# Attention to the first 512 tokens: value products split between the windows and the sums of v; third chunk reads keys that are already on chip

## The chip, the cores and the metric

The kernel runs on one core of a Trainium2 chip. The metric is the device time of one execution in microseconds (us). The engines are TensorE (PE, its weight loads shown apart as PEld), VectorE (DVE), ScalarE (ACT), GpSimd (POOL) and SyncE (SP). Here SP issues all the DMAs. Each engine works through its own list of instructions in order; semaphores make one wait for another.

## The reference

Attention over a local window and over block summaries, then a softplus feed-forward. Everything is float32.

```python
# q, k, v: (4, 8, 768, 64); w_in: (512, 2048); w_out: (2048, 512)
block, window = (32, 16)
nb = S // block                                                   # 24 blocks
k_sum = k.reshape(B, H, nb, block, D).max(axis=3)
v_sum = v.reshape(B, H, nb, block, D).mean(axis=3)
scores_l = scale * np.matmul(q, k.transpose(0, 1, 3, 2))          # masked to |i - j| < 16
scores_s = scale * np.einsum('bhsd,bhnd->bhsn', q, k_sum) + np.log(block)
...
a = softmax(np.concatenate([scores_l_m, scores_s], axis=-1))
x = np.matmul(a, np.concatenate([v, v_sum], axis=2))              # to (3072, 512)
h = x @ w_in
out = (np.maximum(h, 0.0) + np.log1p(np.exp(-np.abs(h)))) @ w_out
```

## The kernel before

**Tiling.** The 3072 tokens (4 batches of 768) are 12 chunks of 256. Heads go in pairs (`hp`, four of them), two heads on the 128 partitions; a unit of attention is one chunk and two head pairs (`NG = 2`), so there are two units a chunk. Within a unit there are 4 windows of 64 queries; each sees 96 keys around it (`KW`) and the 24 summaries (`NB`) of its batch, 120 in all (`KS`).

**A unit of attention** (`attention`): PE makes scores (`sc`, L582), DVE adds the mask and finds maxima (L595), ACT takes exponentials (L603), DVE inverts the sums (L610, L611), DVE or POOL normalizes (L616), the probabilities are transposed into `pT`, and PE multiplies them with v into `xo` (L673). ACT and DVE then write `xo` as a high and a low part, `xh` and `xl` (L689, L693).

**The first two chunks** (512 tokens of batch 0) are done before all else, by `FirstPlaces`, with `by_pe` true: their transposes are made on PE (`pt`, L629) and copied by ACT into `pT` (L633). Their keys lie on chip whole (`kf`, `Sums.declare_first`), so scores are made in two pieces, 96 columns from the keys and 24 from the block maxima `ks`. The sums of v are made on PE (`vt`, L403) and scaled by ACT into 24 rows at partitions 96 to 119 of `vn` (L416). The tile of v for these units, `first`, holds for each window the 96 rows of v at partitions 0 to 95; a DMA for each head pair (`load_sums`, L536) spreads the 24 rows of sums, once for each of the 8 windows, to partitions 96 to 119 of `first`. A value product then takes all 120 rows at once. `vs` is a second copy of the sums, by four small DMAs (`keep_first`, L422), for the third chunk.

**All later chunks** use `Places`: windows of k and v are loaded by DMA for each unit (L474, L483), the maxima are copied behind the keys of each window by DVE or ACT (L490), the sums of v are loaded by DMA (L500), and the transpose goes through DVE and a DRAM buffer `squares` (L642, L650, L654). The third chunk, the last of batch 0, is among these.

**The feed-forward** takes groups of two chunks (the third and the last chunk alone). For each of 16 slices `f` of the hidden width PE makes `ph` (L804), ACT the softplus (L824, L828), DVE the low part `gl` (L832), PE the product with w_out into `po` (L841). The weights are split into a high and a low part on chip, by some eight steps on DVE, ACT and POOL for each slice (L735 to L775). The buffers of the 16 slices serve as scratch first: 6 and 7 hold `vn`, 8 to 11 `first`, 14 and 15 the resident keys `kf`. At the start PE also runs 40 products without use (`warm`, L915).

**The order.** Every step is a task with an index. `SEQUENCE` lists the tasks in the order of their issue; this order is each engine's list, SP's DMAs included. A letter behind an index names another way of doing it (another engine). The numbers in `order.add` (an engine and a time) served to make the sequence; at run time only the sequence counts.

Of the kernel before, what the change touches and what calls it, by code (L numbers as in the profile page):

```python
# [10 lines left out]
F32 = mybir.dt.float32  # L11
# [136 lines left out]
2 160 43 45 68 64 51 133 0 53 161a 3 151 4 44 5 6 162 46 47 7 165a 100 163 72 164 49 166 55 8 73 1 9 167 96 10  # L148
11 138 142 134a 168 74 84 135 57 136 137 52 59 85 139 12 54 101 152a 132 61 75 13 86 140a 14 66 76a 50 141a 70
56 48 77 156 65 15 153 16 69 154 143a 104 189 87 147 144 145 78 79 146 190 17 80 58 155 105 148 60 62 149 88a 63  # L150
116 106 67 150a 18 117 71 19 157 20 21 169 22 23 170 24 158a 25 98 118 26 159 102 27 28 107 29 108a 30 97 31 103
32 33 191 99 81 195 192 179 89 180 193 91 90 34 194 92 35 199 82 119 93 171a 83 196 388 94 109 36 128 95 110 111
37 120a 112 129 38 197 390 172 113 391 175 198 131 121 130 123 122 173 39 124 40 389 174 41 114 200 42 125 181a
387 115 176 309 126 185 127 182 396a 310 219 177 183 220 184 239 318 311 240 178 319 312 186 313 399 320 321 314
414 201a 209 315 187a 415 325 188 210 413 205 202 229 269 203 221a 204 316 225 317 249 222 326 322 206 400 331
417 289 245 223 207 416 224 323 230 332 333 208 327 290 324 226 328 241a 334 337 279 227 242 259 243 401 329 244
228 343 422a 402 211a 403a 338 330 212 213 425 214 344 335 345 246 404 339 215 336 340 405 602 235 426 341 216
247 346 427 342 248 347 217a 584 604 218 348 392 393 395 349 394 428 588 429 406 585 397 231a 408 355 407 398
350 232 409 233 603 234 250 351 353 356 589 236 357 352 586 610a 605 358 410 601 430 237 354 418 419 411 238 359
424 431 412 251a 270 587a 361 423 255 252 590 253 613 362 254 432 367 420 614 434 256 363 421 435 433 364 615  # L160
628 360 257a 365 258 591a 594 366 373 368 598 616 260 369 371 374 370 375 595a 436 376 599 592 372 437 280 275
438 378 377 439 617 381a 382 593 383 379 440 627 441 445 265 630 442 606 271 631 380 446 295 272 451 273 447 596
274 443 452 299 453 444 629 448 276 449 454 457 597 277 463 458 278 450 459 464 455 465 460 636a 456 384 261 461
385 262 469 386 608 466 263 639 470 618 285 475 654 471 264 655 619 462 476 653 472 467 266 477 640 291a 468 473
478 474 641 481 292 658 267a 487 293 294 479 482 600 661 296 483 480 675 488 485 484 676 489 300 490 493 297 268
620 677 623 499 642 494 622 643a 680a 495 281a 486 298a 496 491 644 508 662 645 500 282 305 492 283 683 509 284
501 497 804 510 502 607 286 301a 498 511 805 516 609 621 612 663 302 806 287a 504 288 512 503 303 812a 522 304
517 505a 306 506a 518 513 523 507 519 807 514 524 611 307 528 525 803 664 308 665a 515 666 534 542 529 530 667
531 684 624 520 685 632 635 646 637 815 633 634 521 649 648 526 647 625 638 535 626 830 527 686 832 687a 546 532
536 831 833 537 688 650 550 651 668 656 652 657 533 551 816 671 838a 660 552 556 669 553 670 541 557 659 558 539  # L170
817 559 689 538 548 829 562 543 544 540 545 672 554 818 678 673 819a 690 555 563 679 841 691 547 681 564 560 565
692 674 693 561 682 566 820 549 568 857 574 569 570 571 567 575 694 576 577 572 695 808 814 696 573 578 873 842
811 697 809 810 858a 580 821 705 698 855 699 843 700 581 701 702 822 579 874 711 582 825 823 706 844 583 845a
872 876 856 875 703 712 813 704 713 707 709 708 859 714 717 846 847 867 824 723 718 860 861 710 724 719 715 725
720 868 716 881 865 862a 721 726 729 884 730 731 826 732 866a 722 827 834 848 735 869 835 828 849 885 863 837
851 727 736 899 836 737 840 886 738 728 839 870a 741 901 850 902 864 900 898 907 733 742 887 888a 747 743 744
889 753 748 749 734 910 750 852 911 739 877 740 754 853 745 755 912 756 871 746 854 882 759 890 879 913 765 760
914a 891 915 880 761 893 762 892 751 883 894 878 771 766 916 767 752 757 768 895 772 773 758 903 896 904 897 763
906 774 917 918 919 764 920 905 769 908 909 770 1031 1035 1032 775 1030 776 921 777 1033 922 1034 923 1036 1037
783 778 779 780 789 784 785 786 924 790 791 792 1038 932 1039 1053 1054 1052 1057 1040 781 782 787 925 1041 1042  # L180
788 926 793 933 927 794 934 797a 795 798 1043 796 799 928 800a 801 1044 929 935 802 938 930 939 931 940 1045
1060 941 1046 1047 1048 936 1061 937 1062 942 943 1049 1063 944 1055 1050 1064a 1074 1075 1083a 1051 1077 1065
1076 1078 950 945 1056 1066 1058 946 1059 947 948 951 952 953 1086 956 1067 1087 1068 1069 1070 1088 962 949 957
954 1089 1090a 1091 958 955 963 960 959 1092 964 1100 965 1101 1109a 961 1071 968 1072 1079 1081 1073 1093 1094
1095 1096 974 969 1080 1082 970 1084 971 1085 980 975 1103 1102 976 1104 977 1097 966 1105 1098 1107 1099 1106
1108 1112 981 1110 982 1111 967 1113 1232 972 1236 983 1114 973 978 979 984 1115 1116a 1117 985 986 1233 1118
1237 1234 1238 992 987 1119 1120 988 1121 989 1122 990 993 994 995 998 1235a 1239a 1242 1004 999 1000 1246 1001
1249 1250 1258 1251 1010 1005 1253 1006 1252 1243 991 996 1247 1007 1240 1016 1011 1012 1244 1248 1241 1261 997
1262 1002 1013 1263 1245 1003 1008 1009 1017 1014 1264 1265a 1266 1018 1015 1123 1019 1267 1275 1276 1284 1020
1124 1277 1021 1024 1125 1279 1278 1022 1025 1254 1023 1027 1026 1126 1268 1028a 1269 1270 1271 1029 1255 1134  # L190
1127 1257 1256 1128 1259 1129 1260 1287 1135 1136 1130 1288 1131 1132 1137 1289 1133 1138 1272 1139 1280 1281
1273 1290 1140 1283 1291a 1282 1285 1274 1286 1292 1146 1141 1293 1302 1306 1303 1142 1301 1143 1144 1147 1148
1149 1294 1152 1295 1296 1297 1158 1153 1154 1155 1298 1159 1160 1309 1304 1299 1305 1300 1307 1145 1310 1308
1150 1161 1311 1151 1156 1157 1162 1312 1313a 1163 1314 1164 1315 1324 1328 1325 1323 1170 1165 1316 1166 1317
1318 1167 1168 1171 1319 1172 1173 1176 1320 1177 1178 1331 1326 1321 1179 1327 1322 1329 1169 1332 1330 1174
1333 1175 1180 1181 1182 1334 1335a 1336 1188 1183 1337 1184 1185 1186 1189 1190 1191 1338 1194 1339 1340 1341
# [5 lines left out]
1477 1464 1478 1486a 1401 1480 1479 1465 1481 1399 1400 1402 1407 1466 1467a 1468 1403 1405 1404 1408 1469 1409  # L202
1410 1406 1413 1470 1471 1472 1473 1411 1414 1415 1416 1412 1419 1474 1420 1421 1489 1482 1475 1422 1484 1476
1483 1417 1485 1490 1487 1488 1418 1491 1425 1423 1426 1492 1493a 1424 1431 1494 1427 1428 1495 1429 1432 1433
# [788 lines left out]
```

## Time and profile before

| | us |
|---|---|
| median of 3 runs | 642.35 (641.68 to 645.0) |
| the profiled execution | 644.38 |
| its span (first to last instruction) | 642.6 |
| PE busy | 622.6 (97% of the span) |
| ACT busy | 316.6 (49%) |
| DVE busy | 284.2 (44%) |
| POOL busy | 67.2 (10%) |
| chain that ended last: PE, lines L841 and L804 | 38% and 38% |
| chain: PE, lines L673 and L582 | 3% and 3% |

A row of a view names the line, the engine, the operation, `out<-in` by the program's names and the tile's shape, then the count (`x32`). Square brackets at the end of a row of the timeline give the engine's idle time before it and what ended it. A float32 product of the attention shows as two instructions in the trace. The ends of matmuls are modelled, their starts are measured. A row of the windows view gives, for a stretch, the length, then busy time and count of PE, PEld, DVE, ACT and POOL, the granted clock of PE (1.00 is full), the share of time in which the DMA engines were busy, and GB/s.

### The profile page before, as it was taken

Reading aid. Unit: us, or ns where it says so; the run is one execution under the profiler, and the core shown is the slowest. Engines: PE = TensorE matmul, PEld = TensorE weight load, DVE = VectorE, ACT = ScalarE, POOL = GpSimd, SP = SyncE. Lnnn points to the kernel's source line nnn. Section 1 sums busy time; section 2 is a strip of 40 time slices with the busy share of each in tenths; the row PEclk is TensorE's granted clock in tenths of the full one; section 3 lists DMA queues with packets and bytes.
Section 4 is the critical chain, followed back from the end, with each engine's and each line's share of the span. In section 5 each row is a group of like instructions: output and inputs, shape, how many; then the busy total and the mean of one; then the engine's idle time right before and its main releaser. Section 6 shows DMA issues by size and latency. Waiting matters only on the chain.

```text
span 642.6 us, 11188 instructions
## 1 busy us (share of the span) xinstructions
PE 622.6 (97%) x4284; PEld 505.5 (79%) x4284; DVE 284.2 (44%) x763; ACT 316.6 (49%) x760; POOL 67.2 (10%) x62
## 2 busy tenths in 40 slices
PE   5969999999999999999999999999999999999997
PEld 4567768887788888787787787788888887888996
DVE  4967987578745464313451435432311111341111
ACT  3869978479743534525472435452521322552222
POOL 3523441424100000001000030000000000000000
PEclk9979999999999999999999999999999999999999
DMA  9999759736486843451344563453300400311100
GB/s 285 254 231 294 259 169 256 240 119 174 150 231 191 273 118 71 127 136 42 131 139 138 164 146 102 140 156 106 97 1 0 138 1 1 107 46 62 55 1 34
DMA packets 86630, 86.51 MB, mean 135 GB/s; under 512 B 26705, under 2 KB 72369, under 8 KB 86577
## 3 DMA queue, kind: packets, MB, share of 16 engines
q1 hardware_dynamic: 86576, 85.80, 46.3%
q8 instruction: 34, 0.56, 0.4%
q14 instruction: 20, 0.16, 0.1%
HBM read 65.01 MB, written 18.35 MB: 130 GB/s over the span
## 4 chain that ended last, share of the span: by engine, by line
PE 82%; DVE 3%; ACT 2%; DMA 1%; issue 1%; SPq 1%; POOL 0%; DVEq 0%; ACTq 0%; POOLq 0%
PE po L841 38%; PE ph L804 38%; PE xo L673 3%; PE sc L582 3%; ACT sp L603 1%; DVE w L775 1%; DMA raw<-w_in_dram 1%; DVE gl L832 1%; DVE sp L595 0%; DMA pT<-squares 0%; DVE t L750 0%; DVE ss L610 0%; ACT t L738 0%; POOL sp L616 0%; SPq L500 0%
## 5 line engine op out<-in xcount | busy, mean ns | idle before, releaser
L804 PE MATMUL ph<-xh,w 128*128 128x512 f32 (+1 forms) x896 | 261.3, 364 | 1.1 <-DVE gl L832 1.0
L841 PE MATMUL po<-w,gh 128*128 128x512 f32 x768 | 205.1, 396 | 0.0
L804 PEld LDWEIGHTS ph<-xh,w 128*128 128x128 f32 x896 | 161.4, 188 | 32.7 <-DVE gl L832 2.1
L832 DVE TENSOR_TENSOR gl<-ph,gh 128x512 fp32r<-128x512 f32 (+1 forms) x112 | 68.1, 612 | 226.5 <-ACT ph L828 198.4
L841 PEld LDWEIGHTS po<-w,gh 128*128 128x128 f32 x768 | 141.9, 188 | 32.8 <-issue 0.8
L804 PE MATMUL ph<-xl,w 128*128 128x512 f32 (+1 forms) x448 | 162.3, 362 | 0.0
L824 ACT ACTIVATE gh<-ph 128x512 fp32r<-128x512 f32 (+1 forms) x112 | 60.0, 537 | 203.4 <-PE ph L804 167.0
L841 PE MATMUL po<-w,gl 128*128 128x512 f32 x384 | 115.6, 398 | 0.0
L804 PEld LDWEIGHTS ph<-xl,w 128*128 128x128 f32 x448 | 84.3, 188 | 15.0
L841 PEld LDWEIGHTS po<-w,gl 128*128 128x128 f32 x384 | 70.8, 188 | 17.0 <-issue 1.1
L603 ACT ACTIVATE sp<-sp,nm 128x120 f32<-128x120 f32 x192 | 73.1, 384 | 4.3 <-DVE nm L595 4.1
L828 ACT ACTIVATE ph<-ph 128x512 f32<-128x512 f32 (+1 forms) x112 | 59.2, 532 | 0.0
L764 POOL TENSOR_TENSOR t<-t,raw 128x1024 int32<-128x1024 int32 (+1 forms) x18 | 41.8, 2323 | 88.1 <-DVE t L750 29.1
L595 DVE CUSTOM_DVE_ANT_0 sp<-sc,added 128x120 f32<-128x120 f32 x192 | 40.7, 278 | 12.8 <-PE sc L582 12.8
L824 ACT ACT_TABLE_LOAD x24 | 30.8, 1283 | 31.1 <-PE ph L804 29.2
L693 DVE TENSOR_TENSOR xl<-xo,xh 128x512 fp32r<-128x512 f32 x24 | 16.5, 689 | 51.5 <-ACT xh L689 51.5
L603 ACT ACTIVATION_READ_ACCUMULATOR sp<-sp,nm 128x1 f32 x192 | 36.2, 189 | 0.0
L689 ACT CAST xh<-xo 128x512 fp32r<-128x512 f32 x24 | 14.1, 586 | 39.4 <-PE xo L673 39.2
L673 PEld LDWEIGHTS xo<-pT,v 120*64 120x64 f32 x640 | 20.3, 138 | 8.5 <-issue 6.0
L616 DVE TENSOR_TENSOR sp<-sp,ss 128x960 f32<-128x960 f32 x21 | 26.1, 1245 | 0.6
L642 DVE STREAM_TRANSPOSE tb<-sp 128x1024 f32<-128x1024 f32 x20 | 24.8, 1240 | 0.9 <-DMA squares<-tb 0.7
L673 PE MATMUL xo<-pT,v 120*64 120x64 f32 x640 | 23.0, 225 | 1.5 <-DMA pT<-squares 1.5
(59 smaller groups left out, 369.1 us busy)
## 6 DMA issues: line engine op xcount, KB each, us to landing
squares<-tb SPq DMA_DIRECT2D x20, 512.0 KB
pT<-squares SPq DMA_DIRECT2D x80, 128.0 KB
raw<-w_out_dram SPq DMA_DIRECT2D x16, 512.0 KB
raw<-w_in_dram SPq DMA_DIRECT2D x16, 512.0 KB
kf<-kT_dram SPq DMA_DIRECT2D x16, 384.0 KB
out_dram<-ob SPq DMA_DIRECT2D x11, 512.0 KB
q<-qT_dram SPq DMA_DIRECT2D x20, 256.0 KB
st<-v_hp_dram SPq DMA_DIRECT2D x12, 384.0 KB
```

Of the source, the lines that this page charges most:

```text
L582: nc.tensor.matmul(unit(g * NU + h * NPAIR + i)[r * QW:(r + 1) * QW, k0:k1], lhsT=q[rows, w * QW:(w + 1) * QW], rhs=k[rows], start=True, s ...
L595: nc.vector.tensor_tensor_reduce(out=sp()[:, n], in0=unit(n), in1=added()[:, kinds.index((lows[w], lows[w + 1]))], scale=-SCALE, scalar=FL ...
L603: nc.scalar.activation(sp()[:, n], sp()[:, n], AF.Exp, bias=nm()[:, n:n + 1], scale=-1.0, accum_out=ss()[:, n:n + 1],)
L616: engine.tensor_tensor(sp(), sp(), s, op=ALU.mult)
L642: nc.vector.transpose(out=tb().rearrange("p k (u q) -> p u k q", q=SQ), in_=tiles.sp().rearrange("p u (k q) -> p u k q", q=SQ),)
L673: nc.tensor.matmul(xo()[h * D:(h + 1) * D, g * CH + w * QW:g * CH + (w + 1) * QW], lhsT=tiles.v(g)[:, w, h * D:(h + 1) * D], rhs=queries(g ...
L764: nc.gpsimd.tensor_tensor(a, a, word(0, I32), op=ALU.add)
L804: nc.tensor.matmul(ph()[:, :n_x], lhsT=w1()[:, i1, part, cc * P:(cc + 1) * P], rhs=a()[:, cc, :n_x], start=cc == 0 and i == 0, stop=cc == ...
L824: nc.scalar.activation(gh()[:, :n_x], ph()[:, :n_x], AF.Softplus)
L828: nc.scalar.activation(ph()[:, :n_x], ph()[:, :n_x], AF.Softplus)
L832: nc.vector.tensor_sub(out=gl()[:, :n_x], in0=ph()[:, :n_x], in1=gh()[:, :n_x].bitcast(F32),)
L841: nc.tensor.matmul(po[t](), lhsT=a()[:, t * P:(t + 1) * P], rhs=w2()[:, i2, part], start=f == f0 and i == 0, stop=f == f1 - 1 and i == 2,)
```

## The change

Three things are changed, and the sequence with them.

1. **Value products of the first two chunks.** `load_sums` of `FirstPlaces` goes, and with it four DMAs. A product over 120 rows becomes two: one over the 96 rows of the window in `first`, and one over the 24 rows of sums where ACT wrote them, in `vn`, with rows 96 to 119 of `pT`. The second adds to the first in PSUM. A block of 16 products becomes one of 32.
2. **The third chunk's keys.** `Places` has a case `near` for batch 0: no loads of k and no copy of the maxima; scores read `kf` and `ks` in two pieces, as in the first two chunks. The resident keys stay until then, so the loads of weights 14 and 15 come behind the third chunk's scores.
3. **The sequence** is another one throughout.

```diff
@@ class Places
+            near = b == 0
+            k = None if near else buffer([P, NG, NWIN, KS], F32, "k", bufs=1)
...
+            if near:
+                for g in range(NG):
+                    self.k_keys += [sums.kf[hp + g], (sums.k, hp + g)]
+                self.keys = [
+                    [
+                        lambda g=g, s=s: [(0, KW, sums.keys(hp + g)[:, s:s + KW]), (KW, KS, sums.k()[:, hp + g])]
+                        for s in starts
+                    ]
+                    for g in range(NG)
+                ]
...
-            for g in range(NG):
+            for g in range(0 if near else NG):
                 for w, n in runs(starts):
                     self.k_keys.append((k, g, w))
@@ class FirstPlaces
-                def load_sums(g=g):
-                    src = sums.first(hp + g).rearrange("n (o c) -> n o c", o=1)
-                    nc.sync.dma_start(out=v(g)[KW:], in_=src.broadcast_to([NB, n_w, P]))
-                v_keys.append((own[g], "sums"))
-                order.add(SP, 0.4, load_sums, [sums.first_v], [v_keys[-1]], size=12 * KiB * n_w, row=512)
+            v_keys.append(sums.first_v)
...
+                tiles.v_sums = lambda g: sums.first(hp + g)
@@ def attention, values
+                        to = xo()[h * D:(h + 1) * D, g * CH + w * QW:g * CH + (w + 1) * QW]
+                        v, p = tiles.v(g)[:, w, h * D:(h + 1) * D], queries(g, w, h)
+                        if by_pe:
+                            nc.tensor.matmul(to, lhsT=v, rhs=p[:KW], start=True, stop=False)
+                            nc.tensor.matmul(
+                                to, lhsT=tiles.v_sums(g)[:, h * D:(h + 1) * D], rhs=p[KW:], start=False, stop=True,
+                            )
+                        else:
+                            nc.tensor.matmul(to, lhsT=v, rhs=p, start=True, stop=True)
```

PE's list around the first value blocks, before (`xo` are the value products, `pt` the transposes of the next unit, `ph` the feed-forward):

```order
L915 MATMUL warm<-ident 128x128 x16
L673 MATMUL xo<-pT,first 64x64 x16
L629 MATMUL pt<-ident,sp_187 120x128 x8
L915 MATMUL warm<-ident 128x128 x2
L673 MATMUL xo<-pT,first 64x64 x16
```

The same place after the change, from the last warm-up before the first block (L688 is the product over 96 rows, L689 the one over 24; 28 more rows of the block follow in the same turn):

```order
L931 MATMUL warm<-ident 128x128 x6
L688 MATMUL xo<-pT,first 64x64
L689 MATMUL xo<-pT,vn_279 64x64
L688 MATMUL xo<-pT,first 64x64
L689 MATMUL xo<-pT,vn_279 64x64
```

One row of 16 equal products has become 32 rows in turn. Before the fourth block of values the new list has feed-forward products:

```order
L689 MATMUL xo<-pT,vn_279 64x64
L641 MATMUL pt<-ident,sp_342 120x128 x8
L820 MATMUL ph<-xh,w 128x512
L820 MATMUL ph<-xl,w 128x512
L820 MATMUL ph<-xh,w 128x512 x2
L820 MATMUL ph<-xl,w 128x512
L820 MATMUL ph<-xh,w 128x512
L688 MATMUL xo<-pT,first 64x64
```

Before, the fourth block stood behind warm-up products and ahead of all feed-forward.

ACT's list where it writes the sums of v (`vn<-vt`, L416 in both), before (L603 are the exponentials, 8 rows a unit; L633 the copies of the transposes):

```order
L603 ACTIVATE sp_187,ss<-sp_187,nm 128x120 x8
L756 ACTIVATE raw<-raw 128x512
L738 ACTIVATE t<-raw 128x512
L756 ACTIVATE raw<-raw 128x512
L633 COPY pT<-pt 120x512 x2
L768 CAST w<-t 128x512
L416 ACTIVATE vn_264<-vt 24x512
L603 ACTIVATE sp_373,ss<-sp_373,nm 128x120 x16
```

and after (L615 are the exponentials, L645 the copies):

```order
L615 ACTIVATE sp_198,ss<-sp_198,nm 128x120 x8
L772 ACTIVATE raw<-raw 128x512
L645 COPY pT<-pt 120x512
L615 ACTIVATE sp_342,ss<-sp_342,nm 128x120 x16
L416 ACTIVATE vn_279<-vt 24x512
L645 COPY pT<-pt 120x512
L784 CAST w<-t 128x512
L754 ACTIVATE t<-raw 128x1024
```

The sums and one of the two copies that the first value block needs have moved behind the exponentials of all four units.

SP's list, before (`first<-vn` are the spreading DMAs, `raw` the loads of weights):

```order
L531 DMA first<-v_hp_dram 96x128 x2
L722 DMA raw<-w_in_dram 128x4x256
L719 DMA raw<-w_out_dram 128x1024
L536 DMA first<-vn_264 24x8x128 x2
L722 DMA raw<-w_in_dram 128x4x256
```

and after, at the loads of v for the second two head pairs:

```order
L546 DMA first<-v_hp_dram 96x128
L735 DMA raw<-w_out_dram 128x1024
L546 DMA first<-v_hp_dram 96x7x128 x2
L422 DMA vs<-vn_279 24x128
L738 DMA raw<-w_in_dram 128x4x256
```

No row `first<-vn` is left; the loads of v windows are followed by the small copies for the third chunk.

More of the change, by code (lines that the diff above doesn't have):

```diff
@@ L153 @@
[L153 to L162, printed above, removed]
@@ new lines @@
+24 149 114 25 145a 77 150 95 60 151 166 146 62 103 99 26 153 27 63 28 29 78 30 115 96 31 154 116a 79 104a 124
+187a 87 175 155 89 88 188 32 176 90 33 189 34 191 35 36 190 91 126 80 167a 127 192 81 37 195 92 105 196 107 93
+106 38 168 108 39 125 40 171 41 169 42 383 109 170 235 193 172 117 110 119 118 111 305 120 194 173 121 174 177a
+314 122 178 215 181 123 216 236 179 197a 306 225 180 205 390 198 307 265 199 315 182 308 384 309 316 317 388 321
+200 183 389 201 404 184 275 310 202 318 322 206 311 323 391 217a 312 285 313 203a 319 204 226 392 218 327 588
@@ new lines @@
+219 591 220 387 386 237a 393 394a 320 221 325 238 241 222 324 395 328 333 396 239 245 223 240 329 326 334 224
+331 335 242 330 207a 336 411 339 243 208 209 211 244 210 332 570 340 590 337 286 412 212 397 341 399 587 338 342
+413 589 398 343 213a 214 344 571 574 400 345 227 385 246 231 266 228 229 351 230 346 575 232 347 572 348 349 255
+352 414 233 415a 350 251 416 234a 401 353 417 354 355 402 405 403 406 247a 407 573a 357 596a 576 248 418 249 276
+599 358 250 419 408 363 420 600 252 410 359 409 360 356 364 253a 365 254 361 601 577a 580 421 362 369 366 584
@@ new lines @@
+613 602 603a 367 370 581a 368 371 372 422 578 585 614 604 256 374 423 295 375 281 424 373 271 586 425 377 378a
+431 579 426 379 427 616 428 617 376 432 267 605 433 429 261 268 430 291 434 437 269 270 582 443 438 615 439 296
+440 272 435 444 445 606 436 446 441 592 273a 442 449 274 583 455 450 451 380 452 447 257 456 622a 381 448 258
+453 301 382 259 625 457 260 461 640 644a 458 639 262 626 641 467 462 608 463 595 598 454 464 468 459 469 287 627
+460 470 465 288 466 263a 473 264 647 289 277a 628 471 662 290 609 474 479 594 629a 663 661 472 475 278 480 477
@@ new lines @@
+810 795 796 854 799 701 831a 858 704 851 705 862 706 848 800 702 832 809 709 833 707 710 711 852 712 715 708 716
+717 870 718 812 713 820 813 849 814 885 871 822 721 834 855 835 825 886 727 850 722 823 888 723 837 872 724 836
+826 714 884 821 719 887 733 893a 873 728 874a 875 729 720 734 856a 876 735 725 730 857 726 896 838 897 731 839
+863 866 736 898 877 840 868 739 880 864 879 869 745 865 740 899 900a 901 732 746 741 737 902 747 878 742 748 751
+738 752 753 743 754 881 757 889 890 892 903 904 905 744 758 906 891 759 749 894 882 883 895 760 750 1017 1018
@@ new lines @@
+1021 755 1016 756 761 762 907 763 1019 908 1020 909 1022 1023 769 764 765 766 775 770 771 772 910 776 777 778
+1024 918 1025 1039 1040 1038 1043 1026 767 768 773 911 1027 1028 774 912 779 919 913 780 920 783a 781 784 1029
+782 785 914 786a 787 1030 915 921 788 924 916 925 917 926 1031 1046 927 1032 1033 922 1047 1034 923 1048 928 929
+1035 1049 930 1041 1036 1050a 1060 1061 1069a 1037 1063 1051 1062 1064 936 931 1042 1052 1044 932 1045 933 934
+937 938 939 1072 942 1073 1053 1054 1055 1074 1056 948 935 943 940 1075 1076a 1077 944 941 949 946 945 1078 950
@@ new lines @@
+1086 951 1087 1095a 947 1057 954 1058 1065 1067 1059 1079 1080 1081 1082 960 955 1066 1068 956 1070 957 1071 966
+961 1089 1088 962 1090 963 1083 952 1091 1084 1093 1085 1092 1094 1098 967 1096 968 1097 953 1099 1218 958 1222
+969 1100 959 964 965 970 1101 1102a 1103 971 972 1219 1104 1223 1220 1224 978 973 1105 1106 974 1107 975 976 979
+1108 980 981 984 1221a 1225a 1228 990 985 986 1232 987 1235 1236 1244 1237 996 991 1239 992 1238 1229 977 982
+993 1233 1226 1002 997 998 1230 1234 1227 1247 983 1248 988 999 1249 1231 989 994 995 1003 1000 1250 1251a 1252
@@ new lines @@
+1004 1001 1109 1005 1253 1261 1262 1270 1006 1110 1263 1007 1010 1111 1265 1264 1008 1011 1240 1009 1013 1012
+1112 1014a 1254 1255 1256 1257 1015 1241 1120 1113 1243 1114 1242 1245 1115 1246 1273 1121 1122 1116 1274 1117
+1118 1123 1275 1119 1124 1258 1125 1266 1267 1259 1276 1126 1269 1277a 1268 1271 1260 1272 1278 1132 1127 1279
+1288 1292 1289 1128 1287 1129 1130 1133 1134 1135 1138 1280 1281 1282 1283 1144 1139 1140 1141 1284 1145 1146
+1295 1290 1285 1291 1286 1131 1293 1296 1136 1294 1147 1297 1137 1142 1143 1148 1298 1299a 1149 1300 1150 1301
@@ L462, in __init__ @@
             self.q_keys, self.sp_key = [q], (pads, 0)
-            self.k_keys, self.v_keys = [(k, "sums")], []
-            self.keys = [[lambda g=g, w=w: [(0, KS, k()[:, g, w])] for w in range(NWIN)] for g in range(NG)]
+            self.k_keys, self.v_keys = [], []
+            if near:
[9 more added lines that the diff above has]
+            else:
+                self.k_keys.append((k, "sums"))
+                self.keys = [[lambda g=g, w=w: [(0, KS, k()[:, g, w])] for w in range(NWIN)] for g in range(NG)]
             def load_q():
@@ L490, in k_sums @@
                 copy(out=k()[:, :, :, KW:], in_=src.broadcast_to([P, NG, NWIN, NB]))
-            order.add(
-                DVE, 0.31, lambda: k_sums(nc.vector.tensor_copy), [(sums.k, hp + g) for g in range(NG)],
-                [(k, "sums")], port=True, ways=[Way(ACT, 0.36, lambda: k_sums(nc.scalar.copy))],
-            )
+            if not near:
+                order.add(
+                    DVE, 0.31, lambda: k_sums(nc.vector.tensor_copy), [(sums.k, hp + g) for g in range(NG)],
+                    [(k, "sums")], port=True, ways=[Way(ACT, 0.36, lambda: k_sums(nc.scalar.copy))],
+                )
             for g in range(NG):
@@ L516, in v @@
             def v(g):
-                return own[g]()[:KS, n_c * CH:n_c * CH + n_w * P].rearrange("p (w c) -> p w c", c=P)
+                return own[g]()[:KW, n_c * CH:n_c * CH + n_w * P].rearrange("p (w c) -> p w c", c=P)
             q_keys, k_keys, v_keys = [], [], []
@@ L585, in scores @@
                                 )
-        order.add(PE, 1.4 if by_pe else 1.1, scores, [*tiles.q_keys, *tiles.k_keys], [sc])
+        order.add(PE, 1.4 if chunks[c][0] == 0 else 1.1, scores, [*tiles.q_keys, *tiles.k_keys], [sc])
         def sp():
@@ L672, in values @@
                     for h in range(2):
-                        nc.tensor.matmul(
-                            xo()[h * D:(h + 1) * D, g * CH + w * QW:g * CH + (w + 1) * QW],
-                            lhsT=tiles.v(g)[:, w, h * D:(h + 1) * D], rhs=queries(g, w, h),
-                            start=True, stop=True,
-                        )
+                        to = xo()[h * D:(h + 1) * D, g * CH + w * QW:g * CH + (w + 1) * QW]
[4 more added lines that the diff above has]
+                                to, lhsT=tiles.v_sums(g)[:, h * D:(h + 1) * D], rhs=p[KW:], start=False, stop=True,
+                            )
+                        else:
+                            nc.tensor.matmul(to, lhsT=v, rhs=p, start=True, stop=True)
         room = [(xh, "room"), (xl, "room")]
-        order.add(PE, 1.2, values, [pT, *((pT, k) for k in range(NSQ)), *tiles.v_keys, *room], [xo])
+        order.add(PE, 1.9 if by_pe else 1.2, values, [pT, *((pT, k) for k in range(NSQ)), *tiles.v_keys, *room], [xo])
         def of_x(a):
```

57 lines of the change are left out of this document (14 added, 43 removed), and 26 rows, old and new, of the table SEQUENCE.

## The prediction

> **What bounds the kernel now.** The page gives TensorE (PE) 97% of the span, so first I split the span into stages and ask where PE is not full.
>
> ```profile
> core 0: us, PE busy (x) PEld busy (x) DVE busy (x) ACT busy (x) POOL busy (x), PEclk, DMA share, GB/s
> 32.00:50.00 18.00, 12.99 (x171) 12.04 (x172) 10.80 (x15) 11.61 (x23) 4.79 (x2) 0.81 0.99 216
> 50.00:110.00 60.00, 57.57 (x352) 44.98 (x353) 50.65 (x104) 52.70 (x100) 21.23 (x8) 1.00 0.81 251
> 110.00:590.00 480.00, 479.79 (x3105) 387.59 (x3105) 193.48 (x535) 218.62 (x531) 26.93 (x20) 1.00 0.41 119
> ```
>
> From 110 to 590 us PE is never idle; from 50 to 110 it loses 2.4 us. Nothing but PE's own work sets the time there. What remains is the beginning: the feed-forward starts when the first 512 tokens have been attended to, and every microsecond by which that moment moves goes to the end, if the next stage can follow. So the second view is the timeline of PE around that moment, and the third its waits.
>
> ```profile
> 33.30 0.69 PE L673 MATMUL xo<-pT,first 120*64 120x64 f32 x16 [1.57 <-ACT sp L603]
> 34.16 0.98 PE L673 MATMUL xo<-pT,first 120*64 120x64 f32 x16 [0.18 <-issue]
> ...
> 38.89 0.65 PE L629 MATMUL pt<-ident,sp 128*120 128x128 f32 x4
> 39.38 0.39 PE L915 MATMUL warm<-ident 128*128 128x128 f32 x2
> ...
> 44.19 1.65 PE L673 MATMUL xo<-pT,first 120*64 120x64 f32 x32 [3.54 <-DMA first<-vn]
> 45.76 1.96 PE L629 MATMUL pt<-ident,sp 128*120 128x128 f32 x8
> ...
> 49.83 0.50 PE L804 MATMUL ph<-xh,w 128*128 128x512 f32 x1
> ```
> ```profile
> PE xo L673 <- DMA first<-vn: 3.5, 1, 3.5
> PE xo L673 <- DMA pT<-squares: 1.5, 1, 1.5
> ```
>
> The four value blocks (32 instructions each in the trace, two for every product of the program) begin at 33.30; the third waits 3.54 us for the DMA that spreads the sums of v, and the feed-forward begins at **49.83**. That wait is what the change takes away.
>
> ```profile
> 23.41 0.96 SPq L719 DMA_DIRECT2D raw<-w_out_dram  x1
> 27.26 1.88 SPq L536 DMA_DIRECT2D first<-vn  x2
> ...
> 33.88 1.67 SPq L536 DMA_DIRECT2D first<-vn  x2
> ```
>
> These DMAs also stop SP's queue: it stands from 24.37 to 27.26 until ACT has written the sums. The second pair is issued from 33.88 to 35.55 and PE is released at 44.19.
>
> **The change, part by part.** *Start of the first value block.* With no spreading DMA, the block needs the sums themselves, which ACT writes (L416), and the copies of pT.
>
> ```profile
> 23.66 0.58 ACT L633 COPY pT<-pt 120x512 f32<-120x512 f32 x1 [0.80 <-PE pt L629]
> 26.00 0.62 ACT L768 CAST w<-t 128x512 fp32r<-128x512 f32 x1 [1.75 <-POOL t L764]
> 26.64 0.59 ACT L416 ACTIVATE vn<-vt 24x512 f32<-24x512 f32 x1
> ...
> 33.33 1.18 ACT L756 ACTIVATE raw<-raw 128x1024 int32<-128x1024 uint32 x1
> ```
>
> Before, ACT writes them at 26.64 with two of the four softmax blocks still to come, and is through with all of it at 33.33, having idled 0.80 + 1.75 us. The new order puts the sums and one pT copy behind all four, so the same work must be done first: without the two idles it ends at 33.33 - 2.55 = 30.8, and I take **30.7**. Bounds: 27.2, where the sums are ready today (26.64 + 0.59), and 33.3, today's start.
>
> *The products.* A block had 16 products over 120 rows; it has 16 over 96 rows from partition 0 and 16 over 24 rows from partition 96, in turn, each pair adding into one result. The trace shows no such pair. It does show what PE does where neighbours use a different part of its array:
>
> ```profile
> 104.15 0.26 PE L582 MATMUL sc<-k,q 64*64 64x120 f32 x1
> 104.34 0.50 PE L804 MATMUL ph<-xh,w 128*128 128x512 f32 x1
> ```
> ```profile
> 39.27 0.27 PE L629 MATMUL pt<-ident,sp 128*120 128x128 f32 x1
> 39.38 0.39 PE L915 MATMUL warm<-ident 128*128 128x128 f32 x2
> ```
> ```profile
> 115.73 1.15 PE L673 MATMUL xo<-pT,v 120*64 120x64 f32 x32
> 116.81 0.50 PE L841 MATMUL po<-w,gl 128*128 128x512 f32 x1
> ```
> ```profile
> L673 PE MATMUL xo<-pT,v x640: 222/222/271, 96.5 to 590.6; 120*64 120x64 f32 x160
> ```
>
> Where both use the whole array (transpose, then warm-up) the next starts 0.11 us later although the first lasts 0.27. Where the part changes (64x64 to 128x128), the next starts only 0.07 before the first has ended: 104.15 + 0.26 - 104.34. After a value block it is the same: 115.73 + 1.15 - 116.81 = 0.07. So a change of shape lets PE run dry. Inside a block the 32 instructions take 1.08 us, 0.034 each. In the new block the shape changes after every product. A product whose weights could not be loaded ahead lasts 0.271 (the longest in the last row, where a block begins), so the next starts 0.271 - 0.07 = **0.20** later: 32 x 0.20 = **6.4 us a block** against 1.08. Lower bound for a change: 0.222 - 0.07 = 0.15, 4.9 a block; upper: no overlap, 0.27, 8.6. If the two kinds ran on as one shape, the block would take 64 x 0.034 = 2.2. I take 6.4: every change of shape that this trace shows pays.
>
> The Trainium skill, "TensorEngine Tiling (Array Packing)", Key Properties, says that changing the tiling mode, as against the tile, drains the engine; the trace agrees, with 0.19 after a 0.26 us product against 0.11 after a 0.27 us one. It gives no price. The skill speaks the other way too: in "TensorE: Matmul & The Clock Gate", Part 3, matmuls in different groups of 32 rows run beside each other, some 4 ns apart; by that a block would stay near 1.1 us, as an estimate from that page, and the result would lie with the second case below.
>
> *The chain.* PE, then ACT, then PE:
>
> ```profile
> L633 ACT COPY pT<-pt 120x512 f32<-120x512 f32 x8 | 4.7, 584 | 7.2 <-PE pt L629 7.1
> ```
> ```profile
> 57.86 0.39 PE L841 MATMUL po<-w,gl 128*128 128x512 f32 x1
> 58.09 0.40 PE L804 MATMUL ph<-xh,w 128*128 128x512 f32 x1
> ```
>
> Between two blocks stand 8 transposes (39.38 - 38.89 = 0.49 for four, so 0.98, and 0.16 until the last is out) and the last pT copy, 0.58: 1.8 with the handovers. Before the fourth block the new order puts 6 feed-forward matmuls (0.23 apart, 1.4) behind the 0.98 of transposes, which cover the copies; 6 more follow it and cover the writing of xh and xl. So: 30.7, +6.4 +1.8 +6.4 +1.8 = 47.1 for the third block, +6.4 +2.4 +6.4 +1.4 = 63.7, with 12 matmuls (2.8) done by then. The feed-forward stands as if begun at **60.9: +11.1 us**. The wait for the spread sums is gone, but at 47.1 it would have been over.
>
> *Scores of the third chunk.* Its keys come from the resident rows in two pieces, 96 and 24 columns, as the first chunks' do.
>
> ```profile
> 26.59 0.42 PE L582 MATMUL sc<-kf,first 64*64 64x96 f32 x8
> ...
> 27.89 3.84 PE L915 MATMUL warm<-ident 128*128 128x128 f32 x32
> ```
> ```profile
> 55.62 1.05 PE L582 MATMUL sc<-k,q 64*64 64x120 f32 x32
> 56.61 0.73 PE L841 MATMUL po<-w,gh 128*128 128x512 f32 x2
> ```
>
> A split block takes 27.89 - 26.59 = 1.3, a whole one 1.0. Two blocks on a full PE: **+0.6**. All pieces there are 64x64, so no change of shape. Eight key loads and two small copies go; at most two ACT copies of 0.35, and ACT is 52.70 of 60 us busy, so I count nothing (0 to -0.7). The buffers of the resident keys go to weights 14 and 15, needed some 90 us later (11 x 24 and 11 x 12 matmuls at 0.23): nothing.
>
> *The wait at 94.6.* The first value block of the third chunk waited 1.5 us for its pT. In the new order its exponentials and its transpose stand ahead of more of the weights' work, and 180 feed-forward matmuls come before it against 176: I take the wait as gone, **-1.5** (0 if the same queue holds it again).
>
> Sum: 11.1 + 0.6 - 1.5 = **+10.2**. The profiled execution took 644.38 us (span 642.6), which gives 654.6; the median of the runs is 2.0 below it, so **652.5**.
>
> **The rivals.** *The shapes do not cost* (the product over rows 96 to 119 runs beside or right behind the other). Then a block is 2.2, the third could start at 38.7, and the window loads of v, issued until 33.8, hold it until about 40 (they lose 2.9 us of stopped queue and the spreading ahead of them): 40 + 2.2 + 2.4 + 2.2 + 1.4 - 2.8 = 45.4, so -4.4. With +0.6, and the 1.5 given back because the weights come no sooner, -3.8: **638.6**. For it: nothing in the trace has these two shapes. Against it: every other pair of unlike shapes.
>
> *The same, but the wait only changes its name*: the window loads land as late after their issue as the spread sums did (44.19 - 35.55 = 8.6, so 33.8 + 8.6 = 42.4). Then 47.8, -2.0 + 0.6: **641.0**, no change. It decides if the loads are bound by bytes and not by the spreading.
>
> *The clock falls too.* From 32 to 50 us the granted clock was 0.81, and the third block took 1.57 (45.76 - 44.19) against 1.08. A PE that mostly runs dry may count as idle: two blocks at 1.45 of 6.4 add 5.8, **658**. The Trainium skill, "TensorE: Matmul & The Clock Gate", Part 1, says that an idle window of about 3.4 us halves the clock; the trace agrees for waiting, with the 3.54 us wait beside the 0.81, and shows nothing of a PE that drains.
>
> **How the numbers follow.** Shapes cost: 0.66, its own range 646 to 658 (0.15 a change gives 646.4; 0.23 gives 656.4; two microseconds of the start on either side). Clock too: 0.06. Shapes free: 0.19. Free, but windows late: 0.09. About what a measurement of this kernel can tell from no change is 0.5%, 3.2 us. Faster: nearly all of the third case and a ninth of the fourth, 0.18. Same: 0.12. Slower: 0.70. The range must reach down to the free case to leave out no more than two tenths: 639 to 658.
>
> **What would show it.** Right: value blocks of 5 to 7 us each on PE's timeline with starts about 0.2 apart, the wait on the spread sums gone, the first feed-forward matmul past 52 and the tail of the attention near 63; everything behind 110 as full as today, shifted. Wrong: blocks of 2.2 us, and the feed-forward begun near 45. The split scores should take 1.3 us twice. A new wait of PE for weights between 60 and 110 would show that the stage behind could not follow.

## The result and the profile after

| | us |
|---|---|
| changed kernel, median of 4 runs | 685.94 (684.54 to 687.04) |
| kernel before, 4 runs beside it | 643.15 (641.68 to 645.0) |
| ratio | **1.0668**, 95% interval 1.0642 to 1.0695 |
| profiled execution of the changed kernel | 687.04, span 685.2 |

The change makes the kernel slower by 42.8 us. The direction is that of the forecast, 652.5; the size is four times the forecast's 10.2. In the page of the changed kernel two rows of the slices, some 17 us each, belong together:

```profile
PE   5999998999999999999999999999999999999997
...
PEclk9955579999999999999999999999999999999999
```

PE counts as busy in nearly all slices, but in the third to sixth (34 to 103 us) the granted clock is half to 0.7. The timeline of PE (start, length, then the instruction; L688 is the product over 96 rows, L689 the one over 24) shows what it does there:

```profile
30.82 0.33 PE L688 MATMUL xo<-pT,first 96*64 96x64 f32 x2
31.08 0.32 PE L689 MATMUL xo<-pT,vn 24*64 24x64 f32 x2
...
33.89 0.47 PE L688 MATMUL xo<-pT,first 96*64 96x64 f32 x2
34.29 0.47 PE L689 MATMUL xo<-pT,vn 24*64 24x64 f32 x2
...
41.95 1.96 PE L641 MATMUL pt<-ident,sp 128*120 128x128 f32 x8
...
45.98 0.48 PE L688 MATMUL xo<-pT,first 96*64 96x64 f32 x2
...
58.89 0.80 PE L931 MATMUL warm<-ident 128*128 128x128 f32 x2
...
63.45 0.48 PE L688 MATMUL xo<-pT,first 96*64 96x64 f32 x2
...
74.44 1.96 PE L641 MATMUL pt<-ident,sp 128*120 128x128 f32 x8
...
78.64 0.33 PE L688 MATMUL xo<-pT,first 96*64 96x64 f32 x2
...
89.77 0.80 PE L820 MATMUL ph<-xh,w 128*128 128x512 f32 x1
```

The four value blocks stand between these rows: 11.13, 12.91, 10.99 and 11.13 us, 46.2 in all. A product takes 0.256 us from start to start at the beginning (twelve in 33.89 - 30.82) and 0.40 from 33.89 on (34.29 - 33.89). The windows view, cut where the products change their pace, gives the clock beside it (its columns are those of the windows quoted before; the granted clock stands third from the end):

```profile
30.80:33.90 3.10, 3.10 (x26) 2.28 (x25) 3.00 (x7) 1.83 (x3) 0.22 (x1) 1.00 1.10 315
33.90:64.60 30.70, 30.70 (x149) 23.87 (x148) 6.94 (x9) 7.45 (x10) 3.79 (x2) 0.50 0.45 116
64.60:67.90 3.30, 3.30 (x28) 2.43 (x26) 0.00 (x0) 0.00 (x0) 0.98 (x1) 1.00 0.00 0
67.90:95.20 27.30, 27.30 (x125) 19.81 (x124) 8.29 (x9) 7.75 (x9) 1.93 (x1) 0.56 0.13 44
```

The clock halves, although this view counts PE as busy in every microsecond. Cut finer, the last row holds three stretches: 0.50 from 68.0 to 78.2 us, 1.00 from 78.3 to 81.6, and 0.50 again until 95. What PE waited for in the attention and behind it, in us, times and longest:

```profile
PE ph L820 <- DVE gl L848: 3.9, 2, 2.5
PE sc L594 <- DVE nm L607: 1.8, 1, 1.8
```

Neither the wait for the spread sums nor the one for `squares` is there any more.

### The profile page after: what moved, and what is told of

The parts are those of the page before. It is cut to its first block, busy times and chain, and to the rows that moved or that the text cites. A ratio compares the mean times of both kernels' runs of the same rounds, so it can differ in the third digit from the quotient of the medians.

```text
span 685.2 us, 11545 instructions
## 1 busy us (share of the span) xinstructions
PE 669.7 (98%) x4476; PEld 539.8 (79%) x4476; DVE 287.3 (42%) x753; ACT 311.6 (45%) x755; POOL 75.5 (11%) x73
## 4 chain that ended last, share of the span: by engine, by line
PE 81%; DVE 2%; ACT 0%; issue 0%; DVEq 0%
PE po L857 38%; PE ph L820 38%; PE xo L693 3%; PE sc L594 3%; DVE t L758 1%; DVE sp L628 0%; DVE gl L848 0%; DVE w L791 0%; ACT sp L615 0%; DVE t L766 0%; DVE w L784 0%; DVE t L762 0%; ACT ob L892 0%; DVE ss L623 0%; ACT gh L840 0%
## 5 line engine op out<-in xcount | busy, mean ns | idle before, releaser
L820 PE MATMUL ph<-xh,w 128*128 128x512 f32 (+1 forms) x896 | 264.0, 367 | 3.9 <-DVE gl L848 3.9
L615 ACT ACTIVATE sp<-sp,nm 128x120 f32<-128x120 f32 x192 | 73.1, 383 | 5.7 <-DVE nm L607 5.6
L615 ACT ACTIVATION_READ_ACCUMULATOR sp<-sp,nm 128x1 f32 x192 | 36.0, 188 | 0.0
L688 PE MATMUL xo<-pT,first 96*64 96x64 f32 x128 | 27.8, 314 | 0.0
L689 PE MATMUL xo<-pT,vn 24*64 24x64 f32 x128 | 27.4, 308 | 0.0
L693 PEld LDWEIGHTS xo<-pT,v 120*64 120x64 f32 x640 | 20.3, 138 | 6.9 <-issue 6.9
```

The source lines that it names most:

```text
L615: nc.scalar.activation(sp()[:, n], sp()[:, n], AF.Exp, bias=nm()[:, n:n + 1], scale=-1.0, accum_out=ss()[:, n:n + 1],)
L688: nc.tensor.matmul(to, lhsT=v, rhs=p[:KW], start=True, stop=False)
L689: nc.tensor.matmul(to, lhsT=tiles.v_sums(g)[:, h * D:(h + 1) * D], rhs=p[KW:], start=False, stop=True,)
L693: nc.tensor.matmul(to, lhsT=v, rhs=p, start=True, stop=True)
L820: nc.tensor.matmul(ph()[:, :n_x], lhsT=w1()[:, i1, part, cc * P:(cc + 1) * P], rhs=a()[:, cc, :n_x], start=cc == 0 and i == 0, stop=cc == ...
```

## The experiments

**Theory one**: each change between the two shapes lets PE run dry, and a PE that runs dry for most of the time counts as idle, so that the clock halves. **Rivals**: the small product, or adding into the place just written, is slow whatever its neighbours are; or the new order of tasks and the third chunk cost most of it. All experiments but one keep the changed kernel's order and its third chunk and edit the value products of the first 512 tokens (`keys` below is the product over 96 rows, `sums` the one over 24). Each is one run, up to the two that are timed at the end; the kernel before, run once beside them on two chips, gave 647.15 and 642.96, so a few microseconds between two such runs say little.

### Grouped: the same work, two changes of shape a block

```diff
-   for g, w, h: keys(g, w, h, start=True); sums(g, w, h, start=False)
+   for g, w, h: keys(g, w, h, start=g == 0 and w == 0)
+   for g, w, h: sums(g, w, h, start=False)
```

> All 16 products over 96 rows of a block first, then all 16 over 24 rows: two changes of shape a block in place of 32, the same work. Theory one (each change of shape lets PE run dry, and a PE that runs dry counts as idle, so that the clock halves): a block takes 64 x 0.034 = 2.2 us plus two changes, under 3 us, the clock stays at 1.0 inside the blocks, the time is 637 to 645 us. Rival (the product over 24 rows is slow in itself): 16 x 0.256 + 16 x 0.068 = 5.2 us a block at full clock, more at half, 655 to 670 us. Rival (the new order of tasks and the third chunk's split scores cost most of it): the blocks get short, but the time stays above 660 us.

Measured: **640.93 us** (the kernel before, beside it, 647.15). The timeline of its first and last block (L685 is the product over 96 rows, L691 the one over 24):

```profile
31.50 1.15 PE L685 MATMUL xo<-pT,first 96*64 96x64 f32 x32
32.58 1.15 PE L691 MATMUL xo<-pT,vn 24*64 24x64 f32 x32
33.66 1.09 PE L641 MATMUL pt<-ident,sp 128*120 128x128 f32 x8
...
45.57 1.15 PE L685 MATMUL xo<-pT,first 96*64 96x64 f32 x32
46.66 1.15 PE L691 MATMUL xo<-pT,vn 24*64 24x64 f32 x32
47.73 0.50 PE L838 MATMUL ph<-xh,w 128*128 128x512 f32 x1
```

A block takes 33.66 - 31.50 = 2.16 us, each kind 1.08. The same products, on the same data, in the same order of tasks: only the turn differs (and the flags that open a sum, which the next experiment leaves as they were), and 45 us are gone. The order of tasks and the third chunk are the same, so neither can carry them.

### The same turn, one shape

```diff
+   rows 0 to 95 beside the sums of v in vn are set to zero by POOL
-   sums: lhsT = vn rows 96 to 119, rhs = pT rows 96 to 119
+   sums: lhsT = vn rows 0 to 119,  rhs = pT rows 0 to 119
```

> The alternating order and the adding into one place stay, but the second product goes over 120 rows, of which 96 hold zeros: both products have one shape. Theory one (changes of shape): 2.2 us a block, clock 1.0, 637 to 645 us. Rival (a product that adds into the place just written has to wait for the one before): 0.256 to 0.404 us a product as in the changed kernel, 8 to 13 us a block, 680 to 690 us.

Measured: **641.39 us**. The timeline (L687 the window's rows, L693 zeros and sums):

```profile
31.33 0.34 PE L687 MATMUL xo<-pT,first 96*64 96x64 f32 x4
31.50 0.29 PE L693 MATMUL xo<-pT,vn 120*64 120x64 f32 x4
31.61 0.34 PE L687 MATMUL xo<-pT,first 96*64 96x64 f32 x4
```

The two kinds still alternate in each half of the columns and still add into the place just written, yet two products take 0.11 to 0.12 us behind the first two (0.17), a quarter of what they took in the changed kernel. 96 rows and 120 rows change nothing; 96 rows and 24 rows at partition 96 do. Adding in place is not the cost. This run changes the number of rows and the place of the rows together. That the place alone costs nothing shows in the kernel before: the products of its scores go from rows 0 to 63 to rows 64 to 127 and back with one shape, and 32 of their instructions take 0.99 us (55.62 to 56.61 in the view shown in the prediction).

### Only the small shape

```diff
-   keys(g, w, h, start=True); sums(g, w, h, start=False)
+   sums(g, w, h, start=True); sums(g, w, h, start=False)
```

> The products over 96 rows are left out of the first 512 tokens and the one over 24 rows is made twice in their place: 32 products a block, all of the small shape. Theory one: no change of shape inside a block, so 32 x 0.068 = 2.2 us a block at clock 1.0, 637 to 645 us. Rival (a small tile is slow in itself, or counts as idle for the clock): 0.25 to 0.4 us a product, 8 to 13 us a block, 680 to 690 us.

Measured: **640.6 us**. This kernel leaves out the products over 96 rows, so only its time can be used.

```profile
30.93 2.13 PE L691 MATMUL xo<-pT,vn 24*64 24x64 f32 x64
32.99 1.09 PE L641 MATMUL pt<-ident,sp 128*120 128x128 f32 x8
```

32.99 - 30.93 = 2.06 us: the small shape is as fast as the large one, and the clock was 0.999 over the run. It is the change that costs.

### Runs of two, and of four

```diff
-   per window and half:   keys, sums
+   per window:            keys for both halves, sums for both halves        (runs of two)
+   per pair of windows:   four times keys, four times sums                  (runs of four)
```

> Two products over 96 rows (both halves of the columns), then two over 24: 16 changes of shape a block in place of 32. Theory one: a run of two products takes 0.256 + 0.07 = 0.32 us at full clock and about 0.5 at half, 16 runs are 5.2 to 8 us a block against 8.2 to 13: about half of the 43 us go, 657 to 672 us. Rival (the small product is slow in itself): as the changed kernel, 680 to 690 us. Rival (adding into the place just written): the place was left one product earlier, so most of the cost goes, under 655 us.

> Runs of four products of one shape, then four of the other: 8 changes of shape a block. From the runs of one (0.256 us at full clock) and of two (0.263) and the 0.117 that two products take where nothing changes, a run of four takes 0.38 us: 8 x 0.38 = 3.0 us a block if the clock stays at 1.0, and 0.6 us if it halves. Theory one says 641 to 646 us if the clock holds, for then a block is under 1 us longer than with grouped products; if a PE that drains 0.15 of every 0.38 us still counts as idle, the granted clock falls below 0.9 between 32 and 50 us and the time is 646 to 655 us.

Measured: **661.0 us** with runs of two, **647.86** with runs of four. First the runs of two, in the timeline (a run is two products, four instructions) and in the windows view; then the runs of four in the same two views:

```profile
31.25 0.34 PE L685 MATMUL xo<-pT,first 96*64 96x64 f32 x4
31.52 0.33 PE L691 MATMUL xo<-pT,vn 24*64 24x64 f32 x4
31.78 0.34 PE L685 MATMUL xo<-pT,first 96*64 96x64 f32 x4
```
```profile
48.80:52.20 3.40, 3.40 (x54) 2.53 (x54) 0.00 (x0) 0.45 (x1) 2.04 (x1) 0.99 0.00 0
52.20:55.60 3.40, 3.40 (x24) 2.95 (x23) 1.52 (x2) 1.44 (x3) 0.00 (x0) 0.52 0.00 0
```
```profile
31.15 0.45 PE L685 MATMUL xo<-pT,first 96*64 96x64 f32 x8
31.53 0.45 PE L691 MATMUL xo<-pT,vn 24*64 24x64 f32 x8
```
```profile
47.40:50.80 3.40, 3.40 (x66) 2.79 (x64) 1.83 (x2) 1.65 (x3) 0.00 (x0) 1.00 0.02 5
50.80:54.20 3.40, 3.40 (x10) 2.62 (x9) 3.15 (x5) 3.38 (x4) 0.45 (x1) 0.51 0.69 233
```

A run of one takes 0.256 us, of two 0.26, of four 0.38: a fixed price for the run, and 0.117 for each two products more. In the trace the two halves start 7 ns apart and the next two products 52 ns later. In a run of four the last instruction takes 0.22 us, so it starts 0.23 behind the first (0.45 - 0.22), and the other shape starts 0.15 behind that (0.38 - 0.23): this is the drain, against 0.05 inside a run. Runs of two cost what theory one said in all, though a run took 0.26 us where it had reckoned 0.32: from 48.8 to 52.2 us they passed at full clock, and after that stretch the clock stood at 0.52. Runs of four gave the time of its second case without the sign expected for it, for the clock stayed at 1.00 from 32 to 50 us. Three blocks passed at full clock; the fourth ran from 47.21 to 50.24, and from 50.8 to 54.2 the clock was 0.51 while PE worked on feed-forward products. So even 0.15 of drain in 0.38 us can cost the clock, here after 3.0 us of it, and the cost lands on the work that follows. Why the first three blocks, which lie beside transposes and warm-up products, went free was not tested. A second fall in this run, 0.50 from 74.8 to 78.1 us, follows a wait of 2.5 us for `gl` and not a block.

### One part alone, and the other part alone

The kernel before, its order, DMAs and third chunk untouched, with its product over 120 rows made in two:

```diff
-   matmul(to, lhsT=v, rhs=p, start=True, stop=True)
+   matmul(to, lhsT=v[:KW], rhs=p[:KW], start=True, stop=False)
+   matmul(to, lhsT=v[KW:], rhs=p[KW:], start=False, stop=True)
```

> The kernel before with one thing changed: the product over 120 rows is made in two, rows 0 to 95 and rows 96 to 119 of the same buffer, in turn. The DMAs that spread the sums, the order of tasks and the third chunk stay as they were. Theory one (changes of shape, and the clock that falls with them): four blocks of 8 to 13 us in place of 1.1 to 1.6, the wait for the spread sums gone because the third block comes after they have landed, 680 to 692 us. Rival (the order of tasks or the third chunk cost part of the 43 us): 655 to 675 us.

Measured: **682.45 us**, where the kernel before gave 642.96: +39.5 of the 42.8 come with these two lines. And the changed kernel's order and third chunk with the old product and the spreading DMAs:

```diff
-   keys(g, w, h); sums(g, w, h)
+   matmul(to, lhsT=v (120 rows), rhs=pT (120 rows), start=True, stop=True)
+   four DMAs that spread the sums, behind a window load of v
```

> The changed kernel's order of tasks and its third chunk, with the products over 120 rows of before: the four DMAs that spread the sums are issued behind a window load of v, ahead of the first value block. Theory one (the products alone cost the time): blocks of 1.1 us, no fall of the clock but in a wait, and the time beside the kernel before, 640 to 650 us, with the wait for the spread sums back, at another block perhaps. Rival (order or third chunk cost most): above 660 us. What it lies above the grouped products (640.93) is what the spreading DMAs cost in this order.

Measured: **648.97 us**. SP's queue, then PE (L691 is the product over 120 rows here):

```profile
30.97 4.47 SPq L552 DMA_DIRECT2D first<-vn  x4
```
```profile
39.56 1.12 PE L691 MATMUL xo<-pT,first 120*64 120x64 f32 x16 [8.51 <-DMA first<-vn]
40.94 1.12 PE L691 MATMUL xo<-pT,first 120*64 120x64 f32 x16 [0.25 <-DMA first<-vn]
```

The wait for the spread sums is back, at the first block and longer than before: 8.51 us. In this order the spreading costs 8.0 us against the grouped products, and 8.4 against the merged ones below (640.61), which ran on the same chip. That price belongs to this order, where the four DMAs go out from 30.97 us on; the kernel before issues its first two at 27.26, and the timed runs below put it only 1.8 to 3.1 us above the kernels without them. So the purpose of the change was sound, if worth less than 8 us; it is the turn of its products that loses.

### The sums' product made once for four windows, and what beats both kernels

The 24 rows of sums are the same for all windows of a head, so one product can take all four windows:

```diff
-   for g, w, h: sums(g, w, h)                    16 products of 64 columns
+   for g, h:    sums over all four windows       4 products of 256 columns
```

> Grouped, and the sums' product of one head and half made once over the 256 columns of all four windows, which share its weights: 4 products in place of 16. If a block is bound by the columns that stream through, 64 of them in 0.0585 us, its second half still takes 4 x 0.23 = 0.9 us and nothing is gained: within 1.5 us of the grouped products' 640.93. If the number of instructions or of weight loads bounds it, a block is 0.5 us shorter and the time up to 2 us.

Measured: **640.61 us**, the block about as long as before (L702 is the merged product, 33.35 - 32.34 = 1.01 us against 1.08, with 8 instructions in place of 32): the columns bound it, and not the number of instructions.

```profile
31.26 1.15 PE L685 MATMUL xo<-pT,first 96*64 96x64 f32 x32
32.34 1.08 PE L702 MATMUL xo<-pT,vn 24*64 24x256 f32 x8
33.35 1.09 PE L641 MATMUL pt<-ident,sp 128*120 128x128 f32 x8
```

Both were then timed.

> The grouped products once more, timed against the kernel before. One look gave 640.93 us, where the kernel before gave 647.15 on that chip and 642.96 on another. If what the change was to bring is there once the shape changes only twice a block, the feed-forward begins 3.5 us earlier (49.83 - 46.3, with the 12 matmuls done by then): 638.5 to 641.5 us, ratio 0.993 to 0.998. If the first look was a fast chip, the ratio's interval holds 1.

> Grouped, with the sums' product of one head and half made once over 256 columns, timed. The blocks took the same time as the grouped ones (2.1 us), so: the same as the grouped products within 0.1%, 638.5 to 641.5 us. If the fewer instructions help anywhere, it lies 0.2% or more below them.

Measured, beside the kernel before at 643.79 (639.85 to 645.26): grouped **641.95**, ratio 0.9979 (0.996 to 0.9999); merged **640.71**, ratio **0.9959** (0.9945 to 0.9972). Both beat the changed kernel by far. The merged one also beats the kernel before, by 0.28 to 0.55%; for the grouped one the gain is about 0.2%, with an interval that ends just short of no gain, and its 641.95 lies just above the 638.5 to 641.5 expected. Whether merged is better than grouped stays open: the intervals overlap. The grouped runs spread more (640.24 to 644.48 against 640.24 to 641.06). In the trace of the timed grouped kernel PE stood 1.5 us in a block of the small products without a releaser (listed as "issue"); the merged kernel has no such row.

## Why the forecast was right and wrong, step by step

- **Start of the first block**, taken as 30.7: it is 30.82. Right.
- **The price of a product, 0.20, and 6.4 us a block: too small, by 7.2 us in the four blocks.** The mechanism, that every change of shape costs, was right, and the experiments bear it out. But the working took one interval, "0.271 - 0.07", for a product, while a product of this kernel is two instructions, and a run of one pays for both: of the 0.33 us in the row at 30.82 the second has the last 0.22, so it starts 0.11 behind the first, and the next product 0.15 behind that. 0.256 in place of 0.20 makes 8.2 us a block, 32.8 in four against 25.6. That is still inside the bounds given (4.9 to 8.6 a block), but those bounds were all at full clock.
- **"The clock falls too", left out of the sum and kept as a rival of two blocks and 5.8 us, with a chance of 0.06: the step that failed.** The clock was not a separate mishap: with the same products grouped it stood at 1.00 all the while, so the drains made it fall. It took not two blocks but everything from 33.9 to 95 us except two stretches of about 3.4 us, the transposes and feed-forward products between the blocks as well, and cost 21.7 us by the account below. The result lies 33.4 us above the forecast (685.94 - 652.5): 21.7 of the clock, 7.2 of the price of a product, and some 4 of waits behind 110 us make nearly all of it.
- **The reading behind that small chance** was that the clock falls with a wait as long as the 3.54 us. The 0.81 between 32 and 50 us held two half-clock stretches, and the first, in the windows view of the kernel before, follows 3.4 us in which PE was busy for 1.65 and waited at most 1.57 at once:

```profile
30.90:34.30 3.40, 1.65 (x29) 1.38 (x29) 3.26 (x7) 3.40 (x15) 0.00 (x0) 1.00 1.11 258
34.40:37.70 3.30, 3.30 (x27) 3.07 (x23) 1.76 (x4) 1.33 (x4) 1.57 (x1) 0.50 1.21 225
```

  So the trace before already showed a fall without one long wait.
- **The account.** Against the grouped kernel, which has the same order (its four blocks 9.3 us, one of them with a gap of 0.3): the changed kernel's 128 products at 0.256 would be 32.8 us, so the drains cost 23.5. Its blocks took 46.2, so the clock cost 13.4 inside them. Between the blocks lie 12.8 us against 7.0: 5.8 more for the clock. From the last block to the end of the next scores 6.8 against 4.3: 2.5 more. Drains 23.5 and clock 21.7 make 45.2 of the 46.0 between the spans of 685.2 and 639.2. Two small terms remain: the first block starts 0.7 earlier than in the grouped kernel (30.82 against 31.50), and the waits for `gl` are 1.1 longer (3.9 against 2.8).
- **Between two blocks, 1.8 and 2.4**: 4.0 to 4.6 at half clock; 2.1 to 2.4 in the grouped kernel, where PE fills the wait for the copies with 10 warm-up products. Nearly right for a full clock.
- **The wait for the spread sums goes, and would have been over at the third block's new time**: right on both counts. With the products split and the DMAs kept, the old order shows no such wait.
- **Split scores, +0.6**: in the grouped kernel a split block stands from 50.72 to 52.03, 1.3 us, as forecast.
- **The wait on `squares`, -1.5**: gone, as forecast. But PE now waits 3.9 us for DVE's low part `gl` where it waited 1.0, so **"everything behind 110 as full as today"** was wrong by some 4 us: from 110 to 632 us PE idles 4.0 of 522 against 0.2. The kernel before's row of the waits, then the same window of the kernel before and of the changed one:

```profile
PE ph L804 <- DVE gl L832: 1.0, 2, 0.8
```
```profile
110.00:632.00 522.00, 521.79 (x3386) 425.58 (x3385) 200.11 (x550) 230.76 (x564) 26.93 (x20) 1.00 0.38 112
```
```profile
110.00:632.00 522.00, 518.00 (x3370) 418.19 (x3368) 225.74 (x594) 247.72 (x592) 52.59 (x37) 1.00 0.43 124
```

  The grouped kernel waits 2.8 us for `gl` in all, 1.4 of it before 110, so most of this wait comes with the new order; what the other 1.1 us in the changed kernel come from was not traced.
- **"The shapes do not cost", 638.6 with blocks of 2.2**: this is what the kernel does once the shapes stop changing, 640.6 to 641.95. Its condition was false for the change as it was written: products of unlike shape ran neither beside nor right behind each other.
- **The window loads that hold the third block until about 40**: in the merged kernel its third block stopped for 0.43 us, until 40.76, on one of them; in the others it came later for other reasons. They are close to the bound but not the bound.

The Trainium skill, "TensorEngine Tiling (Array Packing)", Key Properties, says that changing the tiling mode drains the engine and moving to another tile of the same mode does not. The runs agree on both: 0.15 us of drain between unlike shapes, and 7 ns between the two halves of one shape. The Trainium skill's "TensorE: Matmul & The Clock Gate", section "A second HAM failure mode: psum-queue depth-cycling", says that many short pauses of PE, and not only one long wait, can make the clock fall. It tells this of a kernel that cycled through PSUM banks, and not of changes of shape. The forecast left that section out; the trace agrees that one long wait is not needed, with 0.50 for 30.7 us in which no wait is listed.

## What to carry to other kernels

A matmul split in two by rows is not one more instruction but a change of shape: put all products of one shape together, or give both the same shape (rows of zeros will do), and have both sides of the sum in long runs. When a forecast lets an engine run dry, price the clock with it, over all that follows as well; the two are one case and not two. And read a busy PE beside its granted clock and the spacing of its starts, since the busy time here said 100% where more than half of it was drain.

## What the runs showed of the hardware that was not expected

- The price is per run and not per product: a run of one took 0.256 us, of two 0.26, since the two halves of the columns go side by side.
- The clock fell after 3.0 us of runs of four (drain 0.15 of 0.38 us), and stood at 0.51 from 50.8 to 54.2, while PE worked on feed-forward products. One such stretch came out of the four blocks. How large the drained share must be was not measured.
- Full clock came back for about 3.4 us at a time in the changed kernel (64.6 to 67.9 and 78.3 to 81.6), each time behind transposes with warm-up or feed-forward products, and fell again inside the next block.
- In the three kernels that ran 64 small instructions a block at full pace (grouped, zeros, only the small shape) PE stopped once, for 0.3 to 1.5 us, near the end of the second block, with nothing listed that it waited for. In all four of their traces a transfer of 16 KB on the DMA queue named "instruction" starts at 35.1 to 36.2 us and ends 1.4 to 1.7 us before PE goes on, so a late load of PE's own instructions is the likeliest cause; this was not tested.
